# A decode attention kernel rewritten around pairs of heads

## Chip, cores and metric

The kernel runs on one core of a Trainium2 chip. The metric is the device time of one execution in microseconds (us), the median of three runs.

## What is computed

Two independent attention blocks, A and B, with one new token each for two batch entries. For each block:

```
q      = x @ wq                      # x [2,1,640], wq [640, 32*192]
scores = q . k_cache * 192**-0.5     # k_cache [2,32,8192,192]
p      = softmax(scores)
o      = p . v_cache                 # v_cache as k_cache
result = o @ wo                      # wo [32*192, 640]
```

The output holds both results side by side, [2,1,1280]. All tensors are bf16. K and V make up 805.3 MB, wq and wo 31.5 MB.

## The kernel before, in words

One unit is one head of one batch entry: 8192 keys of 192 numbers, 64 keys on each of 128 partitions. There are 128 units. K of a unit is one load of 3 MB (24576 B per partition) into one of two buffers `kb`, V into one of three `vb`; both come from the SP queue (sp_k L198, sp_v L207, order in L425 to L455), K a unit ahead of V. A load waits for the last reader of its buffer.

- VectorE (DVE) multiplies K by the broadcast q in two halves (dve_mul, L230).
- TensorE (PE) sums the products over the 192 numbers in groups of 16: 12 matmuls with an identity matrix per half (pe_sum, L295); DVE adds up the last 16 (dve_red, L233).
- DVE takes the maximum per partition (L236), GpSimd (POOL) the maximum over partitions (partition_all_reduce, L220), ScalarE (ACT) forms the bias (L243) and the exponentials with their row sums (L246); a second POOL all-reduce adds the row sums (L224).
- PE multiplies the exponentials by V: 32 matmuls that each hold two keys per partition, so that the output has two useful parts, in rows 0 and 32 (pe_pv, L306).
- ACT copies these parts (L253, L254), PE adds and transposes them with tiny fp32 matmuls (pe_f3, L314), ACT scales them (L260), PE multiplies them by wo (pe_f5, L341).

q of a pair of heads comes from pe_q (L287), whose wq is loaded for 8 heads at a time; wo is loaded for 4 heads at a time, the last two parts into a free K buffer. The order on each engine is written out by slots: in slot u, PE first sums unit u, then places old outputs, and multiplies the values of unit u-1 (`put(pe_tab, u + 1, 2, pe_pv(...))`). So the values of a unit come after the sums of the next one. The last V is loaded in four pieces (VSPLIT). A small class `_Stream` collects each engine's instructions and its waits.

Of the kernel before, what the change touches and what calls it, by code (L numbers as in the profile page):

```python
# [5 lines left out]
ALU = mybir.AluOpType  # L6
ACTF = mybir.ActivationFunctionType
AXL = mybir.AxisListType
# [43 lines left out]
def build_kernel(nc, blocks, out):  # L52
# [3 lines left out]
    assert B == 2 and Dh == 192 and Sk == 8192 and D % 128 == 0 and Hn % 8 == 0  # L56
    T = Sk // 128
    TH = T // 2
    DG = 16
    NJ = Dh // DG  # L60
    DC = D // 128
    NH2 = D // 2
    G = NBLK * Hn
    NU = G * B
    NP = G // 2
    LASTP = NP - 1
    scale = float(Dh) ** -0.5
    NK = 2
    NV = 3
    HQ = 8  # L70
    HO = 4
    NWQ = G // HQ
    NWO = G // HO
    NLATE = 2
    NQ = 8
    NZ = 8
    LEAD = 6
    QW = 2 * Dh
    UQ = HQ * B
    UO = HO * B  # L80

    def unit(u):
        g = u // B
        return g // Hn, g % Hn, u % B, g

    def qg_of(u):
        return 2 * (u // B // 2) + u % B

    def qg_first(qg):
        return 4 * (qg // 2) + (qg % 2)  # L90

    with ExitStack() as es:
# [3 lines left out]

        kb = [sb(f"kb{i}", [128, T, Dh], BF16) for i in range(NK)]
        vb = [sb(f"vb{i}", [128, T, Dh], BF16) for i in range(NV)]
        prod = [sb(f"prod{i}", [128, TH, Dh], BF16) for i in range(2)]
        sc = [sb(f"sc{i}", [128, T], F32) for i in range(2)]  # L100
        mp = [sb(f"mp{i}", [128, 1], F32) for i in range(2)]
        mg = [sb(f"mg{i}", [128, 1], F32) for i in range(2)]
        nb = [sb(f"nb{i}", [128, 1], F32) for i in range(2)]
        pb = [sb(f"pb{i}", [128, TH, 33], BF16) for i in range(2)]
        rs = [sb(f"rs{i}", [128, 1], F32) for i in range(2)]
        qbc = [sb(f"qbc{i}", [128, 2, Dh], BF16) for i in range(NQ)]
        wqs = sb("wqs", [128, DC, HQ * Dh], BF16)
        wos = [sb(f"wos{i}", [128, HO // 2, 3, D], BF16) for i in range(2)]
        xT = [[sb(f"xT{k}_{b}", [128, DC], BF16) for b in range(B)] for k in range(NBLK)]
        xbc = [[sb(f"xbc{k}_{b}", [128, DC, 128], BF16) for b in range(B)] for k in range(NBLK)]  # L110
        o_sb = sb("o_sb", [33, 2, 2, Dh], F32)
        ones33 = sb("ones33", [33, 1], F32)
        ident = sb("ident", [128, 128], BF16)
        lall = [sb(f"lall{i}", [128, 2], F32) for i in range(2)]
        rcT = [sb(f"rcT{i}", [128, 2], F32) for i in range(2)]
        oTz = sb("oTz", [128, NZ, 3, 6], BF16)
        out_sb = [sb(f"out_sb{k}", [4, NH2], BF16) for k in range(NBLK)]
        actd = sb("actd", [128, 2], F32)

        qps = ps("qps", [128, 512], F32)  # L120
        ops = [ps(f"ops{i}", [128, 2, 512], F32) for i in range(2)]
        scps = [ps(f"scps{i}", [128, TH, DG], F32) for i in range(2)]
        outps = ps("outps", [128, 512], F32)
        oTps = qps[:, QW:QW + 6]
# [7 lines left out]
        ksem = [sem(f"ksem{i}") for i in range(NK)]  # L132
        k2sem = {NU - 1: sem("k2sem1")}
        vsem = [sem(f"vsem{i}") for i in range(NV)]
        wqsem = sem("wqsem")
        wosem = [sem(f"wosem{i}") for i in range(2)]
        wlsem = [sem(f"wlsem{i}") for i in range(NLATE)]
        xsem = [sem(f"xsem{k}") for k in range(NBLK)]
        osem = [sem(f"osem{k}") for k in range(NBLK)]

        VSPLIT = {NU - 2: [0, T // 2, T], NU - 1: [0, T // 2, 3 * T // 4, 7 * T // 8, T]}
        vpsem = {(u, i): sem(f"vp{u}_{i}") for u, c in VSPLIT.items() for i in range(len(c) - 1)}

        def key(name, *idx):
            for i in idx:
                if i < 0:
                    return None
            return (name,) + tuple(idx)

        vcount = [0] * NV  # L150
        for u in range(NU):
            reg[("k", u)] = (ksem[u % NK], 16 * (u // NK + 1))
            if u in VSPLIT:
                for i in range(len(VSPLIT[u]) - 1):
                    reg[("vp", u, i)] = (vpsem[u, i], 16)
            else:
                vcount[u % NV] += 1
                reg[("v", u)] = (vsem[u % NV], 16 * vcount[u % NV])
        for u, sm in k2sem.items():
            reg[("kb", u)] = (sm, 16)  # L160
        for w in range(NWQ):
            reg[("wq", w)] = (wqsem, 16 * (w + 1))
        for w in range(NWO):
            i = w - (NWO - NLATE)
            reg[("wo", w)] = (wosem[w % 2], 16 * (w // 2 + 1)) if i < 0 else (wlsem[i], 16)
        for k in range(NBLK):
            reg[("x", k)] = (xsem[k], 16 * B)
            reg[("odone", k)] = (osem[k], 32)

        def dma(out_ap, in_ap, s):  # L170
            return lambda eng: eng.dma_start(out_ap, in_ap).then_inc(s, 16)  # L171

        def sp_x(blk, b):
            return dma(xT[blk][b][:], blocks[blk]["x"][b, 0, :].rearrange("(j c) -> j c", c=DC), xsem[blk])

        def sp_wq(w):
            blk = (w * HQ) // Hn
            h0 = (w * HQ) % Hn
            src = blocks[blk]["wq"].rearrange("(j c) n -> j c n", c=DC)[:, :, h0 * Dh:(h0 + HQ) * Dh]
            return dma(wqs[:], src, wqsem)  # L180

        late = kb[NU % NK][:].rearrange("p t d -> p (t d)")
        WOB = (HO // 2) * 3 * D

        def wo_tile(w):
            i = w - (NWO - NLATE)
            if i < 0:
                return wos[w % 2][:]
            return late[:, i * WOB:(i + 1) * WOB].rearrange("p (pr i n) -> p pr i n", pr=HO // 2, i=3)

        def sp_wo(w):
            blk = (w * HO) // Hn
            h0 = (w * HO) % Hn
            src = blocks[blk]["wo"][h0 * Dh:(h0 + HO) * Dh, :].rearrange("(pr p i) n -> p pr (i n)", p=128, i=3)
            i = w - (NWO - NLATE)
            return dma(wo_tile(w).rearrange("p pr i n -> p pr (i n)"), src, wosem[w % 2] if i < 0 else wlsem[i])

        def sp_k(u, part=None):  # L198
            blk, h, b, g = unit(u)
            src = blocks[blk]["k"][b, h].rearrange("(p t) d -> p t d", p=128)  # L200
            if part is None:
                return dma(kb[u % NK][:], src, ksem[u % NK])
            if part == 0:
                return dma(kb[u % NK][:, 0:TH, :], src[:, 0:TH, :], ksem[u % NK])
            return dma(kb[u % NK][:, TH:T, :], src[:, TH:T, :], k2sem[u])

        def sp_v(u, t0=0, t1=T, sm=None):  # L207
            blk, h, b, g = unit(u)
            src = blocks[blk]["v"][b, h].rearrange("(p t) d -> p t d", p=128)
            return dma(vb[u % NV][:, t0:t1, :], src[:, t0:t1, :], vsem[u % NV] if sm is None else sm)  # L210

        def vcuts(u):
            c = VSPLIT[u]
            return list(zip(c[:-1], c[1:]))

        def xbc_copy(blk, b):
            return lambda eng: eng.tensor_copy(xbc[blk][b][:], xT[blk][b][:].unsqueeze(2).broadcast_to([128, DC, 128]))

        def pool_ar(u):
            return lambda eng: eng.partition_all_reduce(mg[u % 2][:], mp[u % 2][:], 128, bass.bass_isa.ReduceOp.max)  # L220

        def pool_ls(u):
            g, b = u // B, u % B
            return lambda eng: eng.partition_all_reduce(lall[g % 2][:, b:b + 1], rs[u % 2][:], 128,  # L224
                                                        bass.bass_isa.ReduceOp.add)

        def dve_mul(u, hf):
            blk, h, b, g = unit(u)
            q = qbc[qg_of(u) % NQ][:, g % 2, :].unsqueeze(1).broadcast_to([128, TH, Dh])
            return lambda eng: eng.tensor_tensor(prod[hf][:], kb[u % NK][:, hf * TH:(hf + 1) * TH, :], q, ALU.mult)  # L230

        def dve_red(u, hf):
            return lambda eng: eng.tensor_reduce(sc[u % 2][:, hf * TH:(hf + 1) * TH], scps[hf][:], AXL.X, ALU.add)  # L233

        def dve_max(u):
            return lambda eng: eng.tensor_reduce(mp[u % 2][:], sc[u % 2][:], AXL.X, ALU.max)  # L236

        def dve_f2(g):
            s0 = 64 * (g % 2)
            return lambda eng: eng.reciprocal(rcT[(g // 2) % 2][s0:s0 + 64, :], lall[g % 2][s0:s0 + 64, :])  # L240

        def act_nb(u):
            return lambda eng: eng.activation(nb[u % 2][:], mg[u % 2][:], ACTF.Identity, scale=-scale)  # L243

        def act_exp(u):
            return lambda eng: eng.activation(pb[u % 2][:, :, ::32], sc[u % 2][:].rearrange("p (j a) -> p j a", a=2),  # L246
# [309 lines left out]
```

## Time and profile before

| what | value |
|---|---|
| median of three runs | 1979.81 us (1979.8 to 1979.93) |
| span of the profiled execution | 1978.0 us |
| moved by DMA | 837.96 MB, mean 424 GB/s |
| TensorE matmul busy | 84% of the span |
| VectorE busy | 53% |
| mean granted TensorE clock | 0.936 |

The profile gives the span of the profiled execution, from its first to its last instruction; its time outside the span isn't listed. A busy PE in this profile is a row of pipelined matmuls, so 84% isn't 84% of its peak. "K landed" means that the last of the 16 DMA engines has written its part and raised the semaphore.

### The profile page before, as it was taken

To read this page: it belongs to the slowest core of one execution; us is meant where nothing else is said; L and a number is where in the kernel's file an instruction comes from. 1 tells how busy PE (TensorE), PEld (TensorE's weight loads), DVE (VectorE), ACT (ScalarE), POOL (GpSimd) and SP (SyncE) were. 2 spreads that over 40 slices of the span, in tenths; PEclk is the share of its full clock that TensorE was granted. 3 is DMA by queue.
4 is the path that set the end of the run, shared out by engine and by line. 5 is a ranking of instruction groups with operands and counts; after the bars stand their busy time and mean duration, and the time that the engine had idled before them with its cause. 6 is when DMAs were issued, how large, how long until landed. Compare 5 with 4: busy or idle time off the path is not lost.

```text
span 1978.0 us, 18521 instructions
## 1 busy us (share of the span) xinstructions
PE 1651.6 (84%) x8076; PEld 816.4 (41%) x8076; DVE 1056.0 (53%) x706; ACT 191.3 (10%) x647; POOL 121.6 (6%) x269
## 2 busy tenths in 40 slices
PE   5988888879888888888888878888788977988878
PEld 2444444334444344443444434444344433444434
DVE  4554555545555455655555556555555555556552
ACT  0100101001010010010110101001001000010000
POOL 2200000000000000000000000000000000000001
PEclk9999999999999899998999999998999899998988
DMA  9999999999999999999999999999999999999995
GB/s 402 430 429 430 429 430 431 430 429 430 430 429 429 431 429 430 431 428 430 431 429 430 427 431 431 428 431 427 432 431 427 430 430 430 430 431 429 430 405 236
DMA packets 47856, 837.96 MB, mean 424 GB/s; under 512 B 5144, under 2 KB 5152, under 8 KB 14752
## 3 DMA queue, kind: packets, MB, share of 16 engines
q1 hardware_dynamic: 47188, 836.78, 99.0%
q8 instruction: 63, 1.03, 0.2%
q14 instruction: 17, 0.14, 0.0%
q10 hardware_dynamic: 588, 0.01, 0.0%
HBM read 836.77 MB, written 0.01 MB: 423 GB/s over the span
## 4 chain that ended last, share of the span: by engine, by line
DMA 74%; DVE 11%; issue 10%; PE 4%; POOL 0%; ACT 0%; SPq 0%; DVEq 0%
DMA kb<-in_B_k_cache_dram 38%; DMA kb<-in_A_k_cache_dram 35%; DVE prod L230 11%; PE scps L295 2%; PE ops L306 2%; DMA wqs<-in_A_wq_dram 1%; PE qps L287 0%; PE outps L341 0%; POOL mg L220 0%; PE qps L325 0%; DVE sc L233 0%; ACT qbc L266 0%; ACT pb L246 0%; ACT out_sb L270 0%; SPq L171 0%
## 5 line engine op out<-in xcount | busy, mean ns | idle before, releaser
L230 DVE TENSOR_TENSOR prod<-kb,qbc 128x6144 bf16<-128x6144 bf16 x256 | 848.2, 3355 | 530.4 <-DMA kb<-in_B_k_cache_dram 265.7
L295 PE MATMUL scps<-prod,ident 128*128 128x512 bf16 x3072 | 784.5, 414 | 289.7 <-DVE prod L230 289.4
L306 PE MATMUL ops<-vb,pb 128*33 128x384 bf16 x4096 | 716.4, 335 | 11.4 <-DMA vb<-in_A_v_cache_dram 6.8
L295 PEld LDWEIGHTS scps<-prod,ident 128*128 128x128 bf16 x3072 | 306.0, 105 | 753.7 <-DVE prod L230 370.9
L306 PEld LDWEIGHTS ops<-vb,pb 128*33 128x33 bf16 x4096 | 400.7, 100 | 315.4 <-issue 63.3
L233 DVE TENSOR_REDUCE sc<-scps 128x32 f32<-128x512 f32 x256 | 176.7, 690 | 345.0 <-PE scps L295 344.2
L220 POOL PARTITION_ALL_REDUCE mg<-mp x128 | 63.7, 498 | 1710.2 <-DVE mp L236 1282.2
L243 ACT ACTIVATE nb<-mg 128x1 f32<-128x1 f32 x128 | 26.0, 203 | 1369.1 <-POOL mg L220 1369.1
L287 PE MATMUL qps<-wqs,xbc 128*128 128x384 bf16 x320 | 65.5, 337 | 22.7 <-DMA wqs<-in_A_wq_dram 17.3
L314 PEld LDWEIGHTS qps<-ones,o_sb 33*128 33x128 f32 x372 | 67.1, 257 | 13.1 <-issue 13.1
L314 PE MATMUL qps<-ones,o_sb 33*128 33x1 f32 x372 | 69.7, 311 | 0.0
L224 POOL PARTITION_ALL_REDUCE lall<-rs x128 | 53.2, 416 | 116.9 <-ACT pb L246 116.9
L253 ACT ACTIVATE o_sb<-ops 1x384 f32<-1x384 f32 (+1 forms) x65 | 30.8, 475 | 248.6 <-PE ops L306 248.6
L246 ACT ACTIVATE pb<-sc,nb 128x64 bf16<-128x64 f32 x128 | 52.3, 408 | 14.0 <-PE ops L306 9.8
L287 PEld LDWEIGHTS qps<-wqs,xbc 128*128 128x128 bf16 x320 | 26.7, 99 | 56.5 <-issue 20.5
L266 ACT ACTIVATE qbc<-qps 128x384 bf16<-128x384 f32 x64 | 31.4, 490 | 141.7 <-PE qps L287 141.0
L254 ACT ACTIVATE o_sb<-ops 1x384 f32<-1x384 f32 (+1 forms) x65 | 31.0, 476 | 0.8
L236 DVE TENSOR_REDUCE mp<-sc 128x1 f32<-128x64 f32 x128 | 28.2, 220 | 4.4
L341 PE MATMUL outps<-wos,oTz 128*4 128x320 bf16 x168 | 27.4, 299 | 0.0
L246 ACT ACTIVATION_READ_ACCUMULATOR pb<-sc,nb 128x1 f32 x128 | 23.8, 186 | 0.0
L341 PEld LDWEIGHTS outps<-wos,oTz 128*4 128x4 bf16 x168 | 11.9, 84 | 17.6 <-issue 11.9
L240 DVE RECIPROCAL rcT<-lall 64x2 f32<-64x2 f32 x64 | 9.9, 154 | 12.7 <-POOL lall L224 11.7
(21 smaller groups left out, 33.2 us busy)
## 6 DMA issues: line engine op xcount, KB each, us to landing
kb<-in_A_k_cache_dram SPq DMA_DIRECT2D x64, 3072.0 KB, 22.5
vb<-in_A_v_cache_dram SPq DMA_DIRECT2D x64, 3072.0 KB, 29.5
kb<-in_B_k_cache_dram SPq DMA_DIRECT2D x63, 3072.0 KB, 22.5
vb<-in_B_v_cache_dram SPq DMA_DIRECT2D x62, 3072.0 KB, 29.8
wqs<-in_A_wq_dram SPq DMA_DIRECT2D x4, 1920.0 KB, 29.0
wos<-in_A_wo_dram SPq DMA_DIRECT2D x8, 960.0 KB, 24.4
wqs<-in_B_wq_dram SPq DMA_DIRECT2D x4, 1920.0 KB, 29.0
wos<-in_B_wo_dram SPq DMA_DIRECT2D x6, 960.0 KB, 24.4
```

What stands on the lines that cost most here:

```text
L220: return lambda eng: eng.partition_all_reduce(mg[u % 2][:], mp[u % 2][:], 128, bass.bass_isa.ReduceOp.max)
L224: return lambda eng: eng.partition_all_reduce(lall[g % 2][:, b:b + 1], rs[u % 2][:], 128, bass.bass_isa.ReduceOp.add)
L230: return lambda eng: eng.tensor_tensor(prod[hf][:], kb[u % NK][:, hf * TH:(hf + 1) * TH, :], q, ALU.mult)
L233: return lambda eng: eng.tensor_reduce(sc[u % 2][:, hf * TH:(hf + 1) * TH], scps[hf][:], AXL.X, ALU.add)
L246: return lambda eng: eng.activation(pb[u % 2][:, :, ::32], sc[u % 2][:].rearrange("p (j a) -> p j a", a=2), ACTF.Exp, bias=nb[u % 2][:], s ...
L254: return eng.activation(o_sb[32:33, b0:b1, hs, :], ops[hs][32:33, b0:b1, Dh:2 * Dh], ACTF.Identity)
L266: return lambda eng: eng.activation(qbc[qg % NQ][:], qps[:, 0:QW].rearrange("p (a d) -> p a d", a=2), ACTF.Identity)
L287: ins = eng.matmul(qps[:, 0:QW], xbc[blk][b][:, c, :], wqs[:, c, off:off + QW], start=(c == 0), stop=(c == DC - 1))
L295: ins = eng.matmul(scps[hf][:], ident[:], prod[hf][:, :, j * DG:(j + 1) * DG], start=(j == 0), stop=(j == NJ - 1))
L306: ins = eng.matmul(ops[(u // B) % 2][0:33, b, 0:QW], pb[u % 2][:, j, :], vv[:, j, :], start=(j == 0), stop=(j == TH - 1))
L314: ins = eng.matmul(oTps[:, 2 * i + b:2 * i + b + 1], o_sb[:, b, :, :].rearrange("p s (r i) -> p i (s r)", i=3)[:, i, :], ones33[:], start= ...
L341: ins = eng.matmul(outps[0:4, 0:NH2], oTz[:, pp % NZ, i, 2 - 2 * half:6 - 2 * half], wt[:, pr, i, half * NH2:(half + 1) * NH2], start=(fir ...
```

## The change

The unit becomes a pair of heads of one batch entry: 16384 keys, 128 per partition, the first head on partitions 0 to 63 and the second on 64 to 127. There are 64 pairs.

- K and V of a pair are loads of 6 MB with 49152 B per partition, into a ring of three buffers used by both in turn. K of pair i goes where V of pair i-2 was, V of pair i where K of pair i-1 was.
- Both wq are loaded first of all, into two ring buffers and the product buffers; all of q is then computed into `qrow`, and a matmul with a selecting matrix broadcasts q of a pair two pairs ahead.
- The products are made in quarters of 32 keys per partition with two product buffers; the third multiply waits until the first quarter is summed, the fourth until the second is.
- Maxima, biases and exponentials are taken for the two halves of the partitions separately; one POOL all-reduce remains, on two columns. The row sums are added by a matmul with ones (`l`).
- The values of a pair come directly after its own sums, 64 matmuls. ACT and DVE add and scale the two parts, and a matmul with a one-hot matrix places each quarter row in an accumulating PSUM tile (`add_place`).
- wo of both blocks is loaded at the end, behind the last V, in 3 and 8 pieces of falling size, into ring buffers; the products with wo (`add_contract`) follow as the pieces land. The last pairs' loads are ordered K62, K63, V62, V63, and V63 has two halves.

The core of the diff, new lines only (the functions taken out are those shown above):

```diff
+    T = 128
+    TQ = T // 4
+    WA = [(0, 19, 1, 0), (19, 38, 1, 19), (38, 48, 2, 0)]
+    WB = [(0, 14, 2, 10), (14, 24, 2, 24), (24, 32, 0, 0), (32, 38, 0, 8), (38, 43, 0, 14), (43, 46, 0, 19),
+          (46, 47, 0, 22), (47, 48, 0, 23)]
...
+        ring = [sb(f"ring{i}", [128, RW], BF16) for i in range(3)]
+        prod = [sb(f"prod{i}", [128, TQ * Dh], BF16) for i in range(2)]
...
+        for blk in range(NBLK):
+            w = blocks[blk]["wq"].rearrange("(j c) n -> j (c n)", c=DC)
+            s = next_slot()
+            load(("wq", blk), s, ring[s][:], w[:, 0:RW], [])
+            reg[("wq5", blk)] = (psem[blk], 16)
+            load_on(prod[blk][:, 0:N], w[:, RW:RW + N], psem[blk])
+            free[s] = [("pr", blk, NQC - 1)]
...
+        order[-4:] = [("k", NP - 2), ("k", NP - 1), ("v", NP - 2), ("v", NP - 1)]
+        for kind, i in order:
+            s = next_slot()
...
+                load((kind, i), s, ring[s][:], src, free[s])
+            free[s] = [("m", i, 3)] if kind == "k" else [("pv", i)]
...
+        def add_mul(i, qd):
+            q = qt[i % 3][:].unsqueeze(1).broadcast_to([128, TQ, Dh])
+            prev = before(i, qd, 2)
+            w = [("k", i), ("qt", i)]
+            w += [("s",) + prev] if prev else [("pr", 0, NQC - 1), ("pr", 1, NQC - 1)]
+            S_dve.add(lambda eng: eng.tensor_tensor(pr3(qd), quarter(i, qd), q, ALU.mult), waits=w, sig=("m", i, qd))
...
+        def add_max(i):
+            def fn(eng):
+                eng.tensor_reduce(mp[i % 2][0:64, 0:1], sc[i % 2][0:64, :], AXL.X, ALU.max)
+                return eng.tensor_reduce(mp[i % 2][64:128, 1:2], sc[i % 2][64:128, :], AXL.X, ALU.max)
...
+            S_pool.add(lambda eng: eng.partition_all_reduce(mg[i % 2][:], mp[i % 2][:], 128, bass.bass_isa.ReduceOp.max),
+                       waits=[("mx", i), key("nb", i - 2)], sig=("ar", i))
...
+        def add_pv(i):
+            S_pe.add(lambda eng: eng.matmul(ops[i % 2][0:2, 448:449], rs[i % 2][:], ones[:], start=True, stop=True),
+                     waits=[("exp", i), key("on", i - 2), ("qe", 1, NQC - 1), ("init",)], sig=("l", i))
...
+                        ins = eng.matmul(ops[i % 2][0:34, 0:2 * Dh], pb[i % 2][:, j, :], vv[:, j, :],
+                                         start=(j == 0), stop=(j == T // 2 - 1))
...
+            def fn(eng):
+                for a in range(4):
+                    at = 128 - (8 * ii + a)
+                    ins = eng.matmul(oall[:, sec:sec + WR], place[:, at:at + 128], on[i % 2][:, a * WR:(a + 1) * WR],
+                                     start=(ii == 0 and a == 0), stop=(ii == PB - 1 and a == 3))
...
+        for i in range(NP):
+            tail = i >= NP - 2
+            add_mul(i, 0)
+            add_mul(i, 1)
+            add_sum(i, 0)
+            if i and i < LAST:
+                add_od(i - 1)
+                add_on(i - 1)
+            add_red(i, 0)
+            add_mul(i, 2)
+            add_sum(i, 1)
+            add_red(i, 1)
+            add_mul(i, 3)
+            add_sum(i, 2)
+            if i and i < LAST:
+                add_place(i - 1)
+            add_red(i, 2)
+            if i + 2 < NP:
+                add_q(i + 2)
+                add_qt(i + 2)
+            add_sum(i, 3)
+            add_red(i, 3)
+            add_max(i)
+            add_exp(i)
+            if not tail:
+                add_pv(i)
```

## The prediction

> **What bounds the kernel now.** I read the slices of the page first, then its chain of waits, the groups, the timeline of one unit in mid-run, and the granted clock window by window.
>
> ```profile
> DMA  9999999999999999999999999999999999999995
> ...
> DMA 74%; DVE 11%; issue 10%; PE 4%; POOL 0%; ACT 0%; SPq 0%; DVEq 0%
> ...
> L230 DVE TENSOR_TENSOR prod<-kb,qbc 128x6144 bf16<-128x6144 bf16 x256 | 848.2, 3355 | 530.4 <-DMA kb<-in_B_k_cache_dram 265.7
> L306 PE MATMUL ops<-vb,pb 128*33 128x384 bf16 x4096 | 716.4, 335 | 11.4 <-DMA vb<-in_A_v_cache_dram 6.8
> ```
>
> The transfers fill every slice but the last, the chain is 74% transfer, and the multiply (L230) waits for K. Loads run at 430 GB/s in every 200 us stretch. So only bytes, packets and the two ends count, as long as the compute of one unit fits in its load time. That must now be worked out for pairs. One unit in mid-run:
>
> ```profile
> 1001.33 6.63 DVE L230 TENSOR_TENSOR prod<-kb,qbc 128x6144 bf16<-128x6144 bf16 x2 [3.03 <-DMA kb<-in_B_k_cache_dram]
> ...
> 1008.01 2.76 PE L295 MATMUL scps<-prod,ident 128*128 128x512 bf16 x12 [0.50 <-DVE prod L230]
> ...
> 1010.81 0.69 DVE L233 TENSOR_REDUCE sc<-scps 128x32 f32<-128x512 f32 x1 [2.25 <-PE scps L295]
> 1011.54 0.22 DVE L236 TENSOR_REDUCE mp<-sc 128x1 f32<-128x64 f32 x1
> 1011.85 0.35 POOL L220 PARTITION_ALL_REDUCE mg<-mp  x1 [12.12 <-DVE mp L236]
> 1012.23 0.20 ACT L243 ACTIVATE nb<-mg 128x1 f32<-128x1 f32 x1 [8.80 <-POOL mg L220]
> 1012.47 0.41 ACT L246 ACTIVATE pb<-sc,nb 128x64 bf16<-128x64 f32 x1
> ```
>
> Columns are start and duration. Twelve summing matmuls take 2.76 us; from the last reduce to the end of the exponential it is 2.07 us. Meanwhile PE places older outputs (L314) and goes on to the values; in the old order it also sums unit u+1 ahead of the values of u, so this latency is covered.
>
> Two more rows matter. Early in the run K is ahead, so a multiply follows the maximum at once, and the all-reduce, 0.35 us elsewhere, lasts as long as the multiplies:
>
> ```profile
> 56.39 6.60 DVE L230 TENSOR_TENSOR prod<-kb,qbc 128x6144 bf16<-128x6144 bf16 x2
> 56.50 6.71 POOL L220 PARTITION_ALL_REDUCE mg<-mp  x1 [3.91 <-DVE rcT L240]
> ```
>
> And the granted clock falls to half for single windows of 3.41 us (the column after POOL's count):
>
> ```profile
> 1010.48:1013.90 3.42, 3.42 (x21) 2.79 (x20) 0.91 (x2) 1.07 (x5) 0.73 (x2) 1.00 0.99 424
> 1013.90:1017.31 3.41, 3.41 (x13) 1.62 (x12) 0.00 (x0) 0.00 (x0) 0.00 (x0) 0.51 1.04 447
> ```
>
> I counted the windows of the trace: none in which matmuls ran for under 40% was followed by full clock; 47 of the 64 falls between them follow such quiet windows (up to 45%), 16 follow the tiny fp32 matmuls of L314, which fill the row but little of the array. A half-clock window that was under about 77% filled was followed by another. A value burst of 32 with one such window takes 7.06 us instead of 5.38, so a full one costs 1.7 us.
>
> **The change: transfers.** Bytes stay: 805.3 MB of K and V, 15.7 of wq, 15.7 of wo. By the trace's list of packets, 24576 B takes 913 ns (median), 3840 B 149 and 3072 B 121: 0.0368 ns per byte plus 7.9 ns per packet. K and V: 128 loads instead of 256, 8 packets per engine each, save 128 x 8 x 7.9 ns = 8.1 us. wq, 5120 packets of 3072 B, now in rows of 12 and 49 KB: 5120 x 121 / 16 = 38.7 us to 36.4. wo, 4096 of 3840 B, now 11 pieces with rows of 1.3 to 24 KB: 38.1 to 36.9. Fewer completion writes (9 ns each): 1.3. Together 12.9 us. The 49152 B packet is not in the trace: the line gives 1817 ns; above, it could cost twice 913, no saving (1826); below, the bare bytes, 1809. I take the line, nearest to the 24576 B row. A pair then takes 16 x 1817 ns + 18 x 9 ns (two completions each) = 29.1 us. All transfers: 64 x 29.1 + 36.4 + 36.9 = 1936 us.
>
> **The ends.** First packet at 1.85 us, as now. Now transfers stand idle 12 us of the last 50 before the last landing at 1969.2, and 8.8 us follow it (L314, L341, output). After the change wo comes last and in ever smaller pieces. SP's waits ahead of them are for the last multiply of pair 63, then the values of 62 and of 63; these end 20 us, 10 us and about 22 us ahead of the moment at which the queue would run empty, so they cost nothing as long as compute lags by less than that. The last piece has one row, so behind the last landing stand two matmuls, one eviction (0.43) and the output (1.75 from issue to the span's end): 3 us. Both wq first: K0 lands at 1.9 + 36.4 + 14.5 = 52.8 us, no loss, as nothing idles in the queue (V0 and K1 wait for the projections, whose 2 x 60 matmuls at 216 to 430 ns and evictions of half a us are done some 15 to 20 us behind their wq, ahead of 52.8 and 67 us). Bounds: 0 to 5 us of delay for the first multiply. Transfers alone: 1.9 + 1936 + 3 = 1941 us.
>
> **The loop.** For pair i PE has s0, s1, s2, placement of i-1, q of i+2, s3, row sum, values of i, in this order, and nothing of i+1 ahead of the values. From PE free (0), with both first multiplies done: s0 to 2.75; reduce 2.79 to 3.48; third multiply 3.51 to 6.87; s2 from 6.92; fourth multiply 7.52 to 10.87; s3 10.93 to 13.68; reduce to 14.41; two maxima over 64 partitions of 128 (0.29 each, estimated from 0.22 for 64) to 15.01; all-reduce 15.10 to 15.45; two biases and two exponentials with their accumulator reads (0.24, 0.24, 0.5, 0.46) to 16.98; fp32 row sum 0.27 (bounds 0.1 to 0.6, L314 at 0.19 a step) to 17.25; 64 value matmuls at 163 ns (31 steps in 5.05 us) 10.43: **27.7 us** at full clock. The old division by POOL's second all-reduce (0.42) is gone; three small DVE operations and one ACT copy (about 1 us) lie ahead of the first reduce, under s0; placement and q lie in the 1.3 us in which PE waits for the fourth multiply.
>
> PE is quiet from 13.68 to 17.25, 3.57 us. A window falls when over 60% of it, 2.05 us, lies in there: 84% of the offsets. Averaged over them the half window costs 1.27 us, and in 21% a second one follows, 0.36. So the loop is 27.7 + 1.6 = **29.3 us**, against 29.1 for the transfers. Bounds: 27.7 (never) and 31.1 (two windows in every pair).
>
> The Trainium skill (TensorE: Matmul & The Clock Gate, "HAM oscillation") warns against idle gaps of PE of over some 3.4 us, since the clock then drops. By that rule each pair pays one window, 29.4 us a pair and 1951 in all. The trace is harsher: gaps of 2.1 us within a window sufficed.
>
> **Putting them together.** K(i+1) goes to the buffer of V(i-1), free at PE's 0 of pair i, and lands no earlier than 0.2 + 1.05 + 14.54 + 0.1 = 15.9 us later (completion of the values, first packet 1.05 us behind an issue as at the start, 8 packets, landing). When it is fresh, it lands 26 us after. So compute can lag 10 us before transfers stand. First values end at 52.8 + 31.6 + 1.6 = 86; pair 61's at 86 + 61 x 29.3 = 1873; then K63's queue, V63 and all of wo, 29.1 + 36.9 + 0.5 + 3 = 69.5: **1943 us** by the loop, 1941 by the transfers. They are equal within what I know, and lag of one adds to the other: I take 1944 for the span. The median shown stands 1.8 us above the profiled span (1979.81 to 1978.0): **1946**.
>
> **Rivals.** *Longer loop.* Each 0.1 us in the loop is 6 us. 29.9 us (one more half window in every third pair) gives 86 + 1824 + 69.5 + 1.8 = 1981, no change; 31.1 gives 2055. For it: the quiet 3.57 us; against: nothing else in the loop is cold.
>
> *All-reduce behind the multiplies* (slower). The maximum ends at 15.0 and K(i+1) lands at 15.9 once the lag is used up. From 0.8 us more in the front part on, m0 of i+1 starts before the all-reduce, which then waits at least 3.3 us; PE is quiet for 7 us and surely goes to half: 33.0 us, and 86 + 2013 + 69.5 + 1.8 = 2170. Once there, it stays. For it: the row of 6.71 us; against: 0.8 us of room and the lag needed. The Trainium skill (SBUF — State Buffer, "Who interferes with whom") states that a DVE operation with two SBUF inputs shuts out a GpSimd one that reads SBUF for its whole duration; by this rule the collision costs all of the multiply, and the trace agrees (6.71 us for two).
>
> *Packets save nothing.* If 49152 B costs twice 913, or as much again is lost to rare slow packets (mean 916), transfers take 9 us more: 1941 + 9 + 1.8 = 1952.
>
> **Numbers.** Forecast, both limits within half a us, 52%; packets save nothing 7%; longer loop 22% (7 still faster, 5 level, 10 slower); blocked all-reduce 19%. Faster 0.66, same 0.05, slower 0.29; a difference under 0.2% can't be told from none here. The range leaves the blocked all-reduce out: from 1935 (no half windows, transfers at the bare bytes, 1941 - 8 + 1.8) to 2055.
>
> **What would show it.** Right: about 433 GB/s until the last slice, a first K at 53 us, 49152 B packets near 1817 ns, values of successive pairs 29.1 to 29.5 us apart, half clock in most value bursts, an all-reduce at 0.35 us, 3 us behind the last landing. Wrong: all-reduces of over 3 us in mid-run, SP waiting long for values with the transfer share under 0.97, or gaps between s0 to s3 longer than 1.5 us.

## The result, and the profile after

The changed kernel takes 1987.84 us (median of four, 1985.05 to 1992.14) against 1979.80: ratio 1.0043, interval 1.0029 to 1.0057. So it is 8 us slower. The prediction said 1946 and faster; 1987.84 lies in its range, but the direction was wrong. The profiled execution has a span of 1985.3 us.

The slices of the page after, clock, transfers and rate:

```profile
PEclk9989989989899989989889899889989889899889
DMA  9999999999999999999999999999999999999999
GB/s 412 437 428 430 439 427 427 426 424 415 413 430 429 410 431 410 432 427 421 416 424 426 419 425 418 420 429 418 421 418 426 421 424 419 423 424 420 415 428 380
```

The share of the DMA engines still reads full, but the rate in mid-run is 410 to 432 GB/s where it was 427 to 432. That contradiction is the first hint. The groups show the same from the other side; the last column is idle time ahead of the group and what ended it:

```profile
L233 DVE TENSOR_TENSOR prod<-ring,qt 128x6144 bf16<-128x6144 bf16 x256 | 852.7, 3352 | 388.2 <-DMA ring<-in_A_k_cache_dram 183.0
...
L281 PE MATMUL ops<-ring,pb 128*34 128x384 bf16 x4096 | 809.4, 367 | 0.0
```

The values (L281) are 13% longer than before in sum (809 against 716 us) and never wait for V. DVE still waits for K, which looks like a kernel bound by its loads. But from the fifth pair on the first multiply of a pair starts 7 to 12 us ahead of the sums that need it, and PE passes from the values of a pair to the sums of the next within 0.1 us, in all pairs but the last two. So PE's own order of work is a closed loop:

```profile
1016.06 5.35 PE L238 MATMUL scps<-prod,ident 128*128 128x512 bf16 x24
1022.88 2.76 PE L238 MATMUL scps<-prod,ident 128*128 128x512 bf16 x12 [1.46 <-DVE prod L233]
...
1026.75 2.76 PE L238 MATMUL scps<-prod,ident 128*128 128x512 bf16 x12 [0.83 <-DVE prod L233]
1033.12 0.19 PE L274 MATMUL ops<-ones,rs 128*2 128x1 f32 x2 [3.61 <-ACT pb L266]
1033.24 11.87 PE L281 MATMUL ops<-ring,pb 128*34 128x384 bf16 x64
1045.05 5.35 PE L238 MATMUL scps<-prod,ident 128*128 128x512 bf16 x24
```

From the first sum to the values it is 17.18 us in every pair in mid-run. The values take 10.57 us at full clock (first start to last end), but in mid-run 11.87, 12.25, 13.40 and 13.50, over and over. The loop is thus 28.98, 29.36, 30.51 and 30.61 us long in turn: 119.47 us for four, which is 35 windows of 3.4133 us. A window is the step in which the granted clock of this trace changes: all its changes lie on one grid of 3.4133 us, to within 4 ns. The granted clock around two of these bursts, on that grid (columns: window and its length, busy us of PE, PEld, DVE, ACT and POOL with their counts, granted clock, DMA share, GB/s):

```profile
1029.09:1032.50 3.41, 0.42 (x2) 0.00 (x0) 1.25 (x3) 1.11 (x5) 0.35 (x1) 1.00 0.80 346
1032.50:1035.92 3.42, 2.80 (x11) 1.41 (x12) 0.00 (x0) 0.56 (x2) 0.00 (x0) 0.50 1.06 460
1035.92:1039.33 3.41, 3.41 (x23) 2.03 (x22) 3.24 (x1) 0.00 (x0) 0.00 (x0) 1.00 1.00 433
1087.12:1090.53 3.41, 0.73 (x4) 0.12 (x2) 1.25 (x3) 0.81 (x4) 0.35 (x1) 1.00 1.03 447
1090.53:1093.94 3.41, 2.47 (x10) 1.25 (x11) 0.00 (x0) 0.86 (x4) 0.00 (x0) 0.50 1.00 432
1093.94:1097.36 3.42, 3.42 (x13) 1.55 (x12) 3.18 (x1) 0.00 (x0) 0.00 (x0) 0.50 1.06 460
1097.36:1100.77 3.41, 3.41 (x23) 2.05 (x22) 3.41 (x2) 0.00 (x0) 0.00 (x0) 1.00 0.87 375
```

A window in which PE ran for 0.42 or 0.73 us is followed by one at half clock. If that one was filled for 2.80 us the clock returns; if only for 2.47, a second follows. Four pairs hold six half windows, the run 96.

### The profile page after: what moved, and what is told of

Same layout as the page of the kernel before. It is cut to its first block, busy times and chain, and to the rows that moved or that the text cites. A ratio compares the mean times of both kernels' runs of the same rounds, so it can differ in the third digit from the quotient of the medians.

```text
span 1985.3 us, 17767 instructions
## 1 busy us (share of the span) xinstructions
PE 1578.6 (80%) x7933; PEld 762.0 (38%) x7933; DVE 1095.1 (55%) x833; ACT 186.9 (9%) x610; POOL 32.2 (2%) x82
## 4 chain that ended last, share of the span: by engine, by line
issue 91%; PE 4%; DMA 3%; DVE 2%; POOL 1%; SPq 0%; ACT 0%; POOLq 0%; DVEq 0%
DMA prod<-in_B_wq_dram 2%; PE ops L281 2%; DVE prod L233 1%; POOL mg L254 1%; PE scps L238 1%; PE ops L205 1%; DMA ring<-in_B_wo_dram 1%; DVE sc L245 0%; SPq L134 0%; ACT pb L266 0%; POOLq L43 0%; DVE mp L251 0%; ACT out_sb L333 0%; PE ops L274 0%; DVE oodd L298 0%
## 5 line engine op out<-in xcount | busy, mean ns | idle before, releaser
L233 DVE TENSOR_TENSOR prod<-ring,qt 128x6144 bf16<-128x6144 bf16 x256 | 852.7, 3352 | 388.2 <-DMA ring<-in_A_k_cache_dram 183.0
L238 PE MATMUL scps<-prod,ident 128*128 128x512 bf16 x3072 | 700.1, 381 | 152.6 <-DVE prod L233 152.6
L281 PE MATMUL ops<-ring,pb 128*34 128x384 bf16 x4096 | 809.4, 367 | 0.0
L281 PEld LDWEIGHTS ops<-ring,pb 128*34 128x34 bf16 x4096 | 440.3, 109 | 346.4 <-issue 138.2
L266 ACT ACTIVATE pb<-sc,nb 64x128 bf16<-64x128 f32 x128 | 81.4, 636 | 3.1
L224 ACT ACTIVATE qt<-qps 64x192 bf16<-64x192 f32 x64 | 20.7, 323 | 566.7 <-PE qps L218 566.7
L254 POOL PARTITION_ALL_REDUCE mg<-mp x64 | 25.8, 404 | 1903.7 <-DVE mp L251 1903.7
L266 ACT ACTIVATION_READ_ACCUMULATOR pb<-sc,nb 64x1 f32 x128 | 38.3, 299 | 0.0
L205 PE MATMUL ops<-ring,xT 128*2 128x512 bf16 x96 | 28.4, 425 | 12.4 <-DMA prod<-in_A_wq_dram 10.5
L298 DVE TENSOR_TENSOR oodd<-ops,oodd 2x192 f32<-2x192 f32 x64 | 22.1, 345 | 12.0 <-ACT oodd L292 12.0
L225 ACT ACTIVATE qt<-qps 64x192 bf16<-64x192 f32 x64 | 20.8, 325 | 0.8
```

Of the source, the lines that this page charges most:

```text
L205: ins = eng.matmul(ops[n % 2][32 * blk:32 * blk + 2, 0:QC], xT[:, c, 2 * blk:2 * blk + 2], src, start=(c == 0), stop=(c == DC - 1))
L224: eng.activation(qt[i % 3][0:64, :], qps[0:64, 0:Dh], ACTF.Identity)
L225: return eng.activation(qt[i % 3][64:128, :], qps[64:128, Dh:2 * Dh], ACTF.Identity)
L233: S_dve.add(lambda eng: eng.tensor_tensor(pr3(qd), quarter(i, qd), q, ALU.mult), waits=w, sig=("m", i, qd))
L238: ins = eng.matmul(scps[qd % 2][:], ident[:], pr3(qd)[:, :, j * DG:(j + 1) * DG], start=(j == 0), stop=(j == NJ - 1))
L254: S_pool.add(lambda eng: eng.partition_all_reduce(mg[i % 2][:], mp[i % 2][:], 128, bass.bass_isa.ReduceOp.max), waits=[("mx", i), key("nb" ...
```

## The experiments

**Theory 1**: the loop on PE binds, and half clock behind the quiet stretch before the values lifts it above the 29.1 us of the transfers. **Theory 2**: the ring of three large buffers binds by itself. Half windows, windows at half clock, are counted over each span (time at half clock divided by 3.413 us).

| run | time, us | ratio to before | half windows |
|---|---|---|---|
| changed kernel | 1987.8 | 1.0043 (1.0029 to 1.0057) | 96 |
| 14 extra matmuls | 1955.0 | 0.9874 (0.9859 to 0.9889) | 5 |
| 7 extra | 1955.0 | 0.9875 (0.9859 to 0.9891) | 36 |
| 5 extra | 1953.5 | 0.9866 (0.9851 to 0.9880) | 38 |
| 3 extra | 1989.7 | 1.0052 (1.0037 to 1.0067) | 97 |
| 6 extra, elsewhere | 1989.8 | 1.0052 (1.0036 to 1.0069) | 98 |
| few values | 1949.6 | 0.9846 (0.9832 to 0.9861) | 248 |
| 14 extra, rows of 24576 B | 1964.7 | 0.9923 (0.9908 to 0.9938) | 3 |
| row sum behind | 1988.2 | 1.0045 (1.0030 to 1.0060) | 96 |
| one operation more | 2040.2 | 1.0300 (1.0283 to 1.0318) | 127 |
| two operations more | 2040.5 | 1.0304 (1.0289 to 1.0320) | 128 |
| sums of the next pair first | 2562.7 | 1.2951 (1.2929 to 1.2973) | 284 |

**Filling the quiet stretch.** PE gets matmuls whose result nobody reads:

```diff
+        warm = ps("warm", [128, 512], F32)
...
+        def add_warm(n):
+            def fn(eng):
+                for j in range(n):
+                    ins = eng.matmul(warm[:], ident[:], ident[:].unsqueeze(1).broadcast_to([128, 4, 128]),
+                                     start=True, stop=True)
...
             add_sum(i, 3)
+            if not tail:
+                add_warm(14)
             add_red(i, 3)
```

> The changed kernel with 14 matmuls of 512 columns (identity by identity, into an unused PSUM bank) on PE behind the last sum of each pair, 3.0 us in the quiet 3.7 us. Theory 1 (the loop on PE binds, and what puts it above the transfers is the half clock that follows the quiet stretch): no half windows in mid-run, value bursts of 10.4 us, a loop of 27.7 us at most, transfers bind, 1943 to 1950 us. Theory 2 (the ring of three large buffers binds: each load of K waits for values and its first packets are slow): added PE work changes nothing, 1980 to 1990 us. Theory 3 (more matmuls draw the clock down or collide): over 1990 us.

Measured: 1955.0 us, 33 us less than the changed kernel and 25 less than before. The clock row and the rate of that run:

```profile
PEclk9999999999999999999999999999999999999999
DMA  9999999999999999999999999999999999999998
GB/s 414 434 432 429 428 432 434 432 433 432 432 433 432 433 431 431 430 432 432 431 433 432 433 432 432 429 433 429 429 430 428 430 434 434 426 432 433 434 421 356
```

The bursts are 10.57 us, the rate is 432 GB/s, and the pairs follow at 29.26 us. More work on PE made the kernel faster; theories 2 and 3 are out. The time is 5 us over the upper end of the expectation; the run with few values says where most of it comes from.

> The same with 7 matmuls, 1.5 us, which leave 2.2 us quiet. Theory 1: a window falls only if nearly all of the 2.2 us lies in it, so in less than half of the pairs; loop 28.4 us, under the 29.1 us of the transfers, 1943 to 1955 us. Theory 2: 1980 to 1990 us.

Measured: 1955.0 us with 36 half windows, the time of the run with 14, which has 5. Once the loop is under the transfers' period, remaining half windows cost nothing.

**Transfers alone**: only every eighth value matmul (`range(j0, j1, 8)`).

> The changed kernel with 8 of the 64 value matmuls of each pair; seven eighths of the values are left out. Theory 1: the loop falls to 20 to 26 us even at half clock, the transfers alone are seen: 1943 to 1948 us, 49152 B packets near 1817 ns in the mean too. Theory 2: if packets of this size or the ring's restarts cost by themselves, packets stay at a mean of about 1847 ns and the time at 1970 us or more.

Measured: 1949.6 us. Half clock now lasts for 43% of the span (248 x 3.413 us), and it doesn't matter:

```profile
PEclk9887778777777778777777678778777878778788
```

The packets average 1822 ns with a median of 1819. So theory 2 fails here also: size and ring by themselves don't slow the loads. The floor is 7 us above the 1943 that I had worked out (1941 for the transfers, 1.8 outside the span): 4.7 are the mean of a packet over 1817 ns (16512 packets x 4.6 ns / 16), and most of the rest is idle time of the queue behind the values of pair 61, 3.8 us here. The run with 14 extra matmuls is 5.4 us longer still: its packets average 1824 ns (16512 x 2.2 ns / 16 = 2.3 us), and its queue stands idle 2.9 us longer in all. Why, no run shows.

**Packet size**: the kernel with 14 extra matmuls, each load in two.

```diff
-                load((kind, i), s, ring[s][:], src, free[s])
+                load_on(ring[s][:, 0:RW // 2], src[:, 0:RW // 2], rsem[s], free[s])
+                rcount[s] += 16
+                load((kind, i), s, ring[s][:, RW // 2:RW], src[:, RW // 2:RW], [])
```

> As the run with 14 matmuls, but each load of K or V is two transfers of 24576 B rows. By the line through the packets (7.9 ns per packet) 127 x 8 packets per engine more cost 8 us plus 1 us of completion writes: 9 us over the run with 14 matmuls, if transfers bind there. If packet size is worth nothing: the same time.

Measured: 1964.7 us, 9.6 more. The line through the packets holds. Of the 25 us that the new structure can gain, 9.6 are packet size; the other 15, by subtraction, would be the fuller rows of wq and wo and the shorter end, which no run takes apart.

**The same work in another place**: 6 matmuls behind the second sum, where PE waits too, but for less than half a window.

> The changed kernel with 6 matmuls of 512 columns (1.3 us) behind the second sum of each pair, where PE waits 1.46 us for the third multiply, not in the quiet stretch ahead of the values. Theory 1: as many half windows as without, 85 to 100, and 1980 to 1992 us. Rival (more PE work anywhere keeps the clock up): few half windows, 1955 to 1965 us.

Measured: 1989.8 us, 98 half windows. So it is the quiet stretch before the values, not PE's amount of work.

**How much filling is needed.**

> 3 matmuls instead of 14 behind the last sum, 0.65 us; 3.1 us stay quiet. Theory 1: the count of half windows lies between those of 0 and 7 matmuls (96 and 36), and the loop still binds or nearly: 1987 - 1.7 x (96 - n) us, not under 1955; for n about 70, 1957 to 1970 us.

> 5 matmuls behind the last sum, 1.1 us; 2.65 us stay quiet. Random offsets: a window falls in 57% of the pairs, the loop is about 28.4 us, the transfers bind, 1955 to 1960 us. Locked loop (pairs stay on 35 windows in 4 as long as the quiet stretch of the same pair falls in the same place): about 97 half windows and 1985 to 1992 us.

Measured: 1989.7 us with 3, all 97 half windows; 1953.5 with 5. With 3 my count of about 70 was wrong, with 5 the locked loop as I put it failed. Between them the run tips. With 3, four pairs still take 35 windows to within 0.01; with 5, the loop is free (28.5 to 30.1 us in mid-run, in no fixed order), and the transfers bind. PE's wait falls from 3.61 to 2.53 us:

```profile
1008.53 1.24 PE L277 MATMUL warm<-ident 128*128 128x512 bf16 x5
1012.31 0.19 PE L283 MATMUL ops<-ones,rs 128*2 128x1 f32 x2 [2.53 <-ACT pb L267]
1012.43 10.57 PE L290 MATMUL ops<-ring,pb 128*34 128x384 bf16 x64
```

This is the fastest full version on record, though its interval overlaps those of 7 and 14 extra matmuls.

**Is the loop locked to the windows?** One or two small ScalarE operations lengthen the way from the all-reduce to the biases:

```diff
             def fn_nb(eng):
+                eng.activation(scr[:, 0 + 2 * i:1 + 2 * i], mg[i % 2][:, 0:1], ACTF.Identity)
                 eng.activation(nb[i % 2][0:64, :], mg[i % 2][0:64, 0:1], ACTF.Identity, scale=-scale)
```

> The changed kernel with one more small ScalarE operation (0.21 us, into a scratch column) between the all-reduce and the biases, so 0.21 us more in the loop and in the quiet stretch. Random offsets: 61 x 0.22 = 13 us more, 2001 us. Locked loop: the period stays at 35 windows in 4 pairs, 1988 us, or jumps to the next ratio, for instance 9 windows per pair (30.7 us), 2040 us; 4 periods divided by 3.4133 us are a whole number.

> Two such operations, 0.42 us more. Random offsets: 27 us more, 2015 us. Locked loop: 1988 us, or 2040 us at 9 windows per pair, and not between.

Measured: 2040.2 and 2040.5 us. Each operation adds only 0.1 us (PE's wait is 3.71 and 3.80 us instead of 3.61): it lasts 0.20 us, but the next operation starts 0.09 to 0.11 us behind its start. By random offsets that is 6 and 12 us. Instead the first costs 52 us and the second nothing: every pair in mid-run takes 30.72 us, 9 windows, with two at half clock. Two pairs of the run with one operation:

```profile
1028.39 0.19 PE L276 MATMUL ops<-ones,rs 128*2 128x1 f32 x2 [3.71 <-ACT pb L268]
1028.51 13.52 PE L283 MATMUL ops<-ring,pb 128*34 128x384 bf16 x64
...
1059.11 0.19 PE L276 MATMUL ops<-ones,rs 128*2 128x1 f32 x2 [3.70 <-ACT pb L268]
```

The burst of the run with two:

```profile
1029.85 13.42 PE L284 MATMUL ops<-ring,pb 128*34 128x384 bf16 x64
```

The front gets 0.1 us longer and the burst 0.1 us shorter, since the half clock ends with the window and not with the work. So lengths are held by the grid, and jump.

> The changed kernel with the fp32 row sum behind the value matmuls instead of ahead, which takes 0.12 us out of the front of the loop. If half windows fall at random offsets the loop is 0.12 us shorter and the time 7 us less, 1980 us. Theory 1 in its present form (the loop and the windows of 3.413 us run locked, 4 pairs on 35 windows) lets the number n of half windows change by itself: the time is then 1987 - 7 - 1.7 x (96 - n) us, wherever n goes.

Measured: 1988.2 us, no change, 96 half windows. This run tells nothing of the lock: moved behind the values, the row sum still stands between two pairs on PE, so the loop didn't get shorter (the first one, whose values run at full clock, is 27.70 us long, in the changed kernel 27.69). That was my mistake in its design.

**The old order**: the first two sums of the next pair ahead of the values, so that the quiet stretch holds useful work. The steps of old outputs (`add_od`, `add_on`, `add_place`) move back accordingly, in lines not shown here.

```diff
             add_sum(i, 0)
+            add_sum(i, 1)
             if i and i < LAST:
-                add_od(i - 1)
-                add_on(i - 1)
+                add_pv(i - 1)
             add_red(i, 0)
...
             add_exp(i)
-            if not tail:
-                add_pv(i)
```

> The order of the old kernel in the new one: the first two sums of pair i+1 stand ahead of the values of pair i, so the quiet stretch is filled with useful work. Theory 1 with the ring: the values of i then wait for K of i+1, and K of i+2 waits for the buffer that these values free, so K to K is 9.3 (two multiplies and sums) + 10.5 (values) + 15.9 (load) = 36 us instead of 29.9, and the time 2250 to 2450 us. Rival (the quiet stretch is all that matters): 1950 to 1960 us.

Measured: 2562.7 us, 39.2 us per pair; above the expectation, in its direction. The bursts are 10.57 us, all at full clock, yet now they stand behind sums that wait for K, and K waits for the values:

```profile
SPq L134 <- PE ops L281: 2393.2, 64, 40.3
```

SP waits for values (L281) nearly all of the time (us in total, times, longest). One K in mid-run:

```profile
1007.22 0.33 SPq L134 DMA_DIRECT2D ring<-in_A_k_cache_dram  x1
...
1025.42 6.63 DVE L233 TENSOR_TENSOR prod<-ring,qt 128x6144 bf16<-128x6144 bf16 x2 [11.24 <-DMA ring<-in_A_k_cache_dram]
1028.84 8.23 PE L238 MATMUL scps<-prod,ident 128*128 128x512 bf16 x24 [15.79 <-DVE prod L233]
```

From the issue of K to the first multiply it is 18.2 us, not 15.9, and the two sums take 8.2 us here (7.1 in the next pair) instead of 5.4, at half clock behind the wait. With these three buffers the old order costs 575 us against the changed kernel's.

## Why the prediction was wrong, point by point

| step | predicted | measured |
|---|---|---|
| 49152 B packet | 1817 ns | 1815 (median) |
| front of the loop | 17.25 us | 17.18 |
| values at full clock, to the next sum | 10.43 | 10.51 |
| half clock per pair | 1.63 | 2.2 |
| loop, mean of the run | 29.3 | 29.86 |
| end of the first values | 86 | 89.4 |
| from pair 61's values to the end | 69.5 | 74.6 |
| span | 1944 | 1985.3 |

- **The step that failed** is the half clock's cost per pair: "84% of the offsets ... 1.27 us, and in 21% a second one follows". It averaged over offsets as if each pair met the grid of windows at random. The loop is a fixed length plus what the windows add, and it settles where it repeats on the grid: 35 windows in four pairs, 1.5 half windows each instead of 1.05. Every pair has one (84% were forecast), and two of the four have a second (21%). 0.56 us x 61 = 34 us of the 42 that are missing. The runs with one and two operations more show that such a loop can't be averaged. That the averaging failed, more than the two thresholds, is an estimate of mine: applied window by window to the measured lengths, a fall under 40 to 45% and a second half window under 75 to 77% give 29.9 to 30.2 us a pair instead of 29.3, and 30.72 with 0.1 us more in front (it is sensitive: with the second threshold at 79% it is 30.72 already without).
- The price of a longer loop, 6 us per 0.1 us, was right: one operation more brought the mean loop from 29.86 to 30.70 us and the time up by 52. The rival of 29.9 us had the loop right; its 1981 is 6 us short, by the start and the end. It had 22% with the longer loops. It should have had more, as forecast and rival differed by 0.6 us in a sum of that accuracy.
- The start was 3.4 us late: K0 has landed at 55.1 us instead of 52.8, and the first multiply waits for the projections of B and begins at 56.7, within the 0 to 5 us allowed.
- The end is 5 us longer. The last data lands 71.5 us behind pair 61's values instead of 66.5. By the packets of the trace 3.2 us of K63's load are still to come at that moment, and the queue stands idle for 1.4 us later on; the sum had 0.5 us beyond V62, V63 and wo, which take 66.9 us together instead of 66.0.
- The blocked all-reduce didn't happen: 0.354 us in the median, and 3.51 us once, in pair 62, where K of 63 is there early and a multiply runs beside it. The room of 0.8 us held.
- Of the signs, 433 GB/s failed (421 to 425 over stretches of 400 us in mid-run), and so did values 29.1 to 29.5 us apart. One sign of being wrong was badly chosen: the transfer share never fell under 0.97 in mid-run, though the loads did slow down.
- In the period of the transfers the prediction writes 18 x 9 ns for two completions. That would be 162 ns and 29.2 us; its 29.1 follows with 2 x 9 ns, one write per engine and load, which is what the trace has.
- The Trainium skill (TensorE: Matmul & The Clock Gate, Part 1) states that the window is 3413 ns long and free-running. The trace agrees: all half windows start on one grid, which lies differently to the start of the span in each run. The warning of the Trainium skill (the same page, "HAM oscillation") of gaps over some 3.4 us is too mild here: 2.5 us of waiting (5 extra matmuls) still gave 38 half windows, though they cost nothing there.

Where the expected gain went: 25 us are there, as the kernel with 14 extra matmuls shows; the loop took 33.

## What to carry to other kernels

When one engine's order of work closes a loop whose length is near the period of the loads, work out that loop with the clock in it, and treat half clock as something that locks: a stretch in which PE waits some 3 us once per round can cost one or two half windows every time. A few matmuls to nowhere in that stretch can bring the loop back under the period of the loads; find the number by trial, since the effect tips (3 did nothing, 5 gained as much as 14). Useful work moved there must not hold a buffer that the next load needs: here that cost far more than it saved.

## What the runs showed of the hardware that was not expected

- A loop can lock to the grid of the clock's windows, and then 0.1 us more costs 52 us and the next 0.1 us nothing.
- A DMA share near 1 can hide slow packets. In the changed kernel 6% of the 49152 B packets took over 5% longer than the median, up to 3.7 us; of these 991, 691 are among the first 32 of the 128 packets of a K load. With 14 extra matmuls it is 0.9%. There a K load is issued 7.3 us (median) ahead of the end of the load before it, in the changed kernel 2.2 us; that the nearly empty queue makes them slow fits, but no run isolates it. The rate shows what the share doesn't, here for the changed kernel and for the one with 14 extra matmuls:

```profile
1000.00:1400.00 400.00, 320.80 (x1593) 155.90 (x1594) 229.33 (x172) 36.19 (x124) 4.96 (x14) 0.91 1.00 423
...
1000.00:1400.00 400.00, 343.02 (x1824) 166.59 (x1823) 227.92 (x177) 36.91 (x126) 4.96 (x14) 1.00 1.00 432
```

- In the run with the next pair's sums first, a K load issued to an emptied queue, with V right behind it, took 18.2 us to the first multiply, where 8 packets alone are 14.5. Of that run's 1055 slow packets 986 are among the first 16 of their load.
